# A fused attention and mixer kernel: idle transposes ahead of the first matmul, values loaded one key tile later, and the first weight loads three slots later

## The chip, the cores and the metric

The kernel runs on 1 core of one Trainium2 chip. The metric is device time in microseconds (us) of one execution; lower is better. Three plain runs give the time, and one further execution was profiled.

## The reference

Inputs q, k, v have the shape (4, 8, 576, 64): 4 batches, 8 heads, 576 tokens. Three stages follow one another.

```python
# 1. attention by positive random features (omega is 128 x 64)
q_s, k_s = q * D**-0.25, k * D**-0.25
def phi(x):
    h = einsum('bhsd,md->bhsm', x, omega) - (x * x).sum(-1, keepdims=True) / 2
    return exp(h - h.max(-1, keepdims=True)) / sqrt(128)
q_p, k_p = phi(q_s), phi(k_s)
kv, z = einsum('bhsm,bhsd->bhmd', k_p, v), k_p.sum(2)
x = einsum('bhsm,bhmd->bhsd', q_p, kv) / (einsum('bhsm,bhm->bhs', q_p, z) + 1e-6)
# 2. x as (4, 576, 512): token mixing, then a channel MLP of width 1536
u = x + (relu(x.T @ w_tok1) @ w_tok2).T
x = u + relu(u @ w_ch1) @ w_ch2
# 3. a 2D Fourier transform mixes x; layer norm; an MLP of width 2048
u = x + real(fft(fft(x, axis=1), axis=2))
out = u + relu(norm(u) @ w_ch1) @ w_ch2
```

## The kernel before

The order of all instructions is written out by hand, and each engine works through its own in that order. A single-precision matmul is made of three fast ones: each operand is split into a rounded high part and the rest.

The first 200 us are the attention stage. The 2304 tokens make 18 tiles of 128 tokens for the keys and 18 for the queries; every tile is worked in two groups of four heads, so `order` in `attention()` has 72 slots. Slots 0 to 9 are key tiles 0 to 4, two slots each; after that a slot of a key tile and a slot of a query tile alternate. In slot n the loop issues, in this order:

- `load`: the transfers of tiles that come up to six slots later, on SyncE's queue (SP). A key tile brings its values (`va`) with it, a split tile two pieces of them. The tiles rotate through three buffers, so a load waits until the tile three before it has been split.
- `project(n)`: six matmuls of 256 columns on TensorE (line 506), the tile's high and low part (`kh`, `kl`) times those of the scaled omega (`om_h`, `om_l`).
- `sums(n)`: for the key slot three before (`LAG`), four matmuls per batch and head with the values (line 540); `queries(n)`: for a query slot, four transposes of the features (line 565).
- `split_in`: the high part of a tile that comes four slots later, a cast on ScalarE (ACT) or for key tiles 1 and 3 on VectorE (DVE), then the low part on GpSimd (POOL), for key tile 0 on VectorE.
- `feature(n)`: the maximum on VectorE (`mx`, line 520), then the exponential on ScalarE (`f`): four activations straight from PSUM (line 524), or a subtraction on VectorE (`df`, line 527) and one wide activation (line 528).
- `results(n)`: numerators on TensorE (line 582) and the division on VectorE (lines 595 to 602).
- `side.step(...)`: work on the side. The later weights arrive in double precision, and `widen` takes each chunk apart into two single-precision parts: a load into `stg`, six wide VectorE operations (lines 341 to 372) and one on ScalarE (`cvy`, line 348), and a store. `weave` puts these items in one list; each item has a cost, each slot adds a budget to a credit, and items are issued while the credit pays for them. The first two loads of the list cost nothing, so they go out with the first step.

The identity for the transposes is made on GpSimd at the start. `bank("H")` hands out the two PSUM banks of that name in turn.

After the attention stage come the token mixing (lines 667 and 680), the channel MLP (lines 776 and 898), the Fourier stage and the last MLP (lines 1457 and 1470).

Of the kernel before, what the change touches and what calls it, by code (L numbers as in the profile page):

```python
# [9 lines left out]
F32 = mybir.dt.float32  # L10
# [10 lines left out]
B, H, S, D, M = 4, 8, 576, 64, 128  # L21
DM = H * D
NTOK = B * S
NT = NTOK // 128
# [2 lines left out]
BLK = 512  # L27

NWB = 3
NBLK = (NTOK + BLK - 1) // BLK  # L30

BLOCKS = [0, NBLK - 1, *range(1, NBLK - 1)]

SLOT0_US, SLOT1_US, SLOT_US, FIRST_US, SHORT_US, CH_US, FF_US, S_US, SAVED_US = 1.2, 0.45, 1.2, 3.9, 1.2, 4.3, 3.8, 1.6, 4.6


NP = NFF // 2
# [11 lines left out]
SPLIT = [i for i in range(NT) if i * 128 // S != (i * 128 + 127) // S]  # L51
# [140 lines left out]
def pieces(t0, n):  # L192

    done = 0
    while done < n:
        b, s = divmod(t0 + done, S)
        step = min(n - done, S - s)
        yield done, step, b, s
        done += step
# [103 lines left out]
def mix_kernel(ctx: ExitStack, tc: tile.TileContext, qt, kt, va, om, w1, w2, wch, wff, t1, t2, out):  # L303
    nc = tc.nc
    pe, act, dve, pool, sync = nc.tensor, nc.scalar, nc.vector, nc.gpsimd, nc.sync
# [7 lines left out]
    ident = const.tile([128, 128], F32, name="ident")  # L313
# [69 lines left out]
    def weave(chunks):  # L383


        items = []
        for i, ((_, done), work) in enumerate(chunks):
            if not i:
                items += [(0.0, chunks[c][0][0]) for c in range(2)] + work[:1]
            items += work[1:6]  # L390
            if i + 1 < len(chunks):
                items.append(chunks[i + 1][1][0])
            if i + 2 < len(chunks):
                items.append((0.0, lambda i=i: side.later(chunks[i + 2][0][0])))
            items.append(work[6])
            items.append((0.0, lambda done=done: side.later(done)))
        return items
# [5 lines left out]
    def slab(j):  # L403
        def store(st, free):
            kept[j] = dram.tile([128, 2, 1024], F32, name="kept")
            side.queue.dma_start(out=kept[j], in_=st["o"].bitcast(F32))
            whole.add(j)
            free()
        return widen(wch[j].bitcast(I32), 1024, store)
# [36 lines left out]
    def bank(tag):  # L446
        if tag not in pools:
            tag = "A"
        if tag == "A" and spare:

            tag = spare.pop(0)
            spare.append(tag)
        pl, bufs = pools[tag]
        return pl.tile([128, 512], F32, tag=tag, name=tag, bufs=bufs)
# [8 lines left out]
    ld = pl.enter_context(tc.tile_pool(name="ld", bufs=3))  # L463
# [5 lines left out]
    def projection():  # L469
        act.dma_start(out=om_sb, in_=om)  # L470
        act.mul(out=om_h, in_=om_sb, mul=scale)
        dve.scalar_tensor_tensor(out=om_l, in0=om_sb, scalar=scale, in1=om_h, op0=ALU.mult, op1=ALU.subtract)

    src = {}

    def load(kind, i):
        t = ld.tile([128, 4, 128], F32, tag="x", name=kind + "s", bufs=3)
        sync.dma_start(out=t, in_=(kt if kind == "k" else qt)[:, i])
        src[kind, i] = t
        if kind == "k":  # L480
            for part, row in enumerate([i] + [NT + c for c, j in enumerate(SPLIT) if j == i]):
                t = ld.tile([128, H, D + 1], F32, tag="v", name="v", bufs=6)
                sync.dma_start(out=t.rearrange("p h d -> p (h d)"), in_=va[row])
                src["v", i, part] = t

    def split_in(kind, i):
        t = src.pop((kind, i))
# [140 lines left out]
    def tok_weights():  # L628
        t1 = w1hl.bitcast(F32).rearrange("p a b c -> p a (b c)")
        t2 = w2hl.bitcast(F32).rearrange("p a b c -> p a (b c)")  # L630

        def done1(st, lo):


            o = st["o"].bitcast(F32)
            sync.dma_start(out=t1[:, :, lo:lo + 640], in_=o[:, :, 0:640])
            sync.dma_start(out=t1[64:128, :, 1280 + lo:1920 + lo], in_=o[0:64, :, 0:640])
            n = min(640, 1024 - lo)
            sync.dma_start(out=t1[0:64, :, 1536 + lo:1536 + lo + n], in_=o[64:128, :, 0:n])
            if n < 640:  # L640
                sync.dma_start(out=t1[0:64, :, 1280:1536], in_=o[64:128, :, n:640])

        def done2(st, lo):
            sync.dma_start(out=t2[:, :, lo:lo + S], in_=st["o"].bitcast(F32)[:, :, 0:S])

        def chunk(w, lo, n, done):
            return widen(w.bitcast(I32)[:, 2 * lo:2 * lo + 2 * n], n, lambda st, free: (done(st, lo), free()))

        return [chunk(w1, 0, 640, done1), chunk(w1, 640, 640, done1), chunk(w2, 0, S, done2), chunk(w2, S, S, done2)]
# [38 lines left out]
    def last_tile(b):  # L688
        return ((b + 1) * S - 1) // 128
# [3 lines left out]
    for b in range(B):  # L693
# [4 lines left out]
        c = [("k", i, g) for i in range(kn, ke) for g in range(2)]  # L698
# [7 lines left out]
    side = Side()  # L706
# [22 lines left out]
    def turns(n, c):  # L729
        return list(range(n)) if c % 2 == 0 else list(range(n))[::-1]  # L730
# [10 lines left out]
    def wait_whole(x):  # L741
        side.until(lambda: x in whole)

    PAIR1 = {(1, p_) for p_ in range(NP)}
    mix = Slots([j for c in range(NBLK) for j in turns(NCH, c)]
                + [(k, p_) for c in range(len(PLAIN)) for p_ in turns(NP, c) for k in (1, 2)],
# [6 lines left out]
    def operand():  # L753
        return [mlp0["ub"].tile([128, 4, BLK], F32R, tag=tag, name=tag) for tag in ("uh", "ul")]
# [26 lines left out]
    def attention():  # L781
        tiles = [(kind, i) for kind, i, g in order if g == (kind == "q")]
        at = {t: order.index(t + (int(t[0] == "q"),)) for t in tiles}
        late = {}
        n_all = len(order)

        def at_slot(n, kind):
            return order[n][1:] if 0 <= n < n_all and order[n][0] == kind else None

        def sums(n):  # L790
            if n in late:
                late.pop(n)()
            if (t := at_slot(n - LAG, "k")) is not None:
                parts = list(pieces(t[0] * 128, 128))
                kv_add(*t, parts[0])
                if len(parts) > 1:
                    late[n + 2] = lambda: kv_add(*t, parts[1])

        def queries(n):
            if (t := at_slot(n - LAG, "q")) is not None:  # L800
                turn(*t)
            t = at_slot(n - LAG_X, "q")
            if t is not None and t[1] == 0:
                turn_x(t[0], at_slot(n - LAG_NUM, "q") != (t[0] + 1, 0))
                for b in range(B):
                    if t[0] == last_tile(b):
                        fill.extend(tok_mix(b))

        def results(n):
            if (t := at_slot(n - LAG_NUM, "q")) is not None:  # L810
                numer(*t)
                divide(*t)
                if t[1] == 0:
                    split_x(t[0])

        loads, splits = list(tiles), list(tiles)
        for n in range(-1, n_all + LAG_X):
            while loads and at[loads[0]] <= n + AHEAD_LOAD:
                load(*loads.pop(0))
            if n == n_all:  # L820
                enter_mlp()
            if 0 <= n < n_all:
                project(*order[n])
            sums(n)
            queries(n)
            while splits and at[splits[0]] <= n + AHEAD_SPLIT:
                split_in(*splits.pop(0))
            if 0 <= n < n_all:
                feature(*order[n])
            results(n)  # L830
            if n >= 2:

                side.step(0.0 if n < 6 else SLOT0_US if n < 10 else SLOT1_US if n < 36 else SLOT_US)
            if fill and (len(fill) > 3 or n % 2 == 0):
                fill.pop(0)()
            for fn in early[:3]:
                fn()
            del early[:3]

    ctx.enter_context(tc.manual_schedule())  # L840
    projection()
    side.rest += weave(tok_weights() + [slab(j) for j in range(NCH)]
                       + [w(p_) for p_ in range(NP) for w in (first, second)])
    attention()
# [9 lines left out]
    wb = pm.enter_context(tc.tile_pool(name="wb", bufs=1, reuse_waits="tile"))  # L854
    mix.free.extend((wb, f"wb{i}") for i in range(NWB))

# [81 lines left out]
    def tables():  # L938
        sync.dma_start(out=t1_sb, in_=t1)
        pool.dma_start(out=t2_sb, in_=t2)  # L940
# [438 lines left out]
    tables()  # L1379
    for at_ in range(1, NBLK):  # L1380

# [8 lines left out]
        v = operand()  # L1390
        last = at_ + 1 == NBLK
        ch_block(at_, BLOCKS[at_], u, ff_prepare(0, v) if last else [lambda: ch_split(BLOCKS[at_ + 1], v)],
# [5 lines left out]
    v = mlp0["ub"].tile([128, 4, BLK], F32R, tag="uh", name="uh")  # L1398
    v = v[:, :, 0:BLK // 2], v[:, :, BLK // 2:BLK]
# [198 lines left out]
```

## Time and profile before

| | us |
|---|---|
| plain runs | 943.9, 944.2, 945.47 |
| median | 944.2 |
| profiled execution, its own time | 946.03 |
| its span, first to last instruction | 943.9 |
| mean granted TensorE clock over the span | 0.998 |

The span is what the trace shows; the profiled execution's own time is 2.1 us longer than its span and 1.8 us longer than the median of the plain runs. Positions in the trace are counted from the start of the span.

### The profile page before, as it was taken

The page shows a single profiled execution, that of the slowest core. Times are in us where ns is not written, and L with a number is a line of the kernel's source. Part 1 is how long each engine was busy: PE and PEld are TensorE (multiplying, and loading weights), DVE is VectorE, ACT ScalarE, POOL GpSimd, SP SyncE. Part 2 cuts the span into 40 slices and gives each one's busy share as a digit, 9 for nine tenths or more (in the row PEclk, how much of TensorE's full clock was granted, in tenths as well). Part 3 has the DMA queues.
Part 4 walks back from the last instruction along what each step waited for, and adds up shares of the span by engine and source line. Part 5 has one row for each costly group of instructions (what it writes and reads, how often), then busy time and mean ns, then how long its engine had stood idle before and what let it go on. Part 6 is the DMA issues. An engine that isn't in the chain of part 4 may idle for free.

```text
span 943.9 us, 14085 instructions
## 1 busy us (share of the span) xinstructions
PE 930.4 (99%) x5344; PEld 830.1 (88%) x5344; DVE 633.2 (67%) x1259; ACT 306.4 (32%) x709; POOL 120.7 (13%) x110
## 2 busy tenths in 40 slices
PE   7999999989999999999999999999999999999998
PEld 7999999978889888888888888889999998899986
DVE  5987999886776787877853667666565557533342
ACT  5886777721212322212221122222311113311121
POOL 3353444221211132011000000000000000000000
PEclk9999999999999999999999999999999999999999
DMA  7765554687897586583145358739766656677764
GB/s 268 231 211 177 184 213 160 252 301 258 345 411 318 174 310 236 180 302 135 60 174 213 134 185 270 240 112 386 268 229 234 227 190 226 227 263 253 249 213 151
DMA packets 68257, 216.47 MB, mean 229 GB/s; under 512 B 5600, under 2 KB 14432, under 8 KB 54240
## 3 DMA queue, kind: packets, MB, share of 16 engines
q1 hardware_dynamic: 60992, 172.40, 52.3%
q0 software_dynamic: 7056, 43.06, 12.3%
q8 instruction: 42, 0.69, 0.3%
q14 instruction: 23, 0.19, 0.1%
q10 hardware_dynamic: 144, 0.13, 0.0%
HBM read 169.30 MB, written 42.47 MB: 224 GB/s over the span
## 4 chain that ended last, share of the span: by engine, by line
PE 97%; DVE 2%; ACT 0%; DMA 0%; issue 0%; DVEq 0%; ACTq 0%
PE H L776 23%; PE A L898 16%; PE A L1470 14%; PE H L1457 12%; PE A L1264 7%; PE A L506 6%; PE H L540 4%; PE N L582 3%; PE A L565 2%; PE A L667 1%; PE A L680 1%; PE S L1077 1%; PE S L1090 1%; PE S L680 1%; PE H L667 1%; PE S L667 1%
## 5 line engine op out<-in xcount | busy, mean ns | idle before, releaser
L776 PE MATMUL H<-uh,w 128*128 128x512 f32 (+1 forms) x800 | 216.3, 356 | 2.1 <-DVE x L683 2.1
L776 PEld LDWEIGHTS H<-uh,w 128*128 128x128 f32 x800 | 137.3, 190 | 22.6 <-DVE x L683 2.3
L860 ACT ACTIVATE hh<-H 128x512 fp32r<-128x512 f32 (+1 forms) x92 | 49.1, 534 | 268.8 <-PE H L776 268.6
L776 PE MATMUL H<-ul,w 128*128 128x512 f32 (+1 forms) x304 | 114.2, 376 | 0.4 <-DVE ul L763 0.4
L898 PE MATMUL A<-hh,w 128*128 128x512 f32 (+1 forms) x480 | 108.7, 369 | 0.0
L1470 PE MATMUL A<-w2t,b 128*128 128x512 f32 x384 | 99.3, 394 | 0.0
L861 DVE SCALAR_TENSOR_TENSOR hl<-H,hh 128x512 fp32r<-128x512 f32 (+1 forms) x92 | 55.8, 606 | 63.8 <-ACT hh L860 63.7
L898 PEld LDWEIGHTS A<-hh,w 128*128 128x128 f32 x480 | 84.2, 188 | 15.0
L1457 PE MATMUL H<-b,w1t 128*128 128x384 f32 x480 | 91.4, 336 | 0.0
L1457 PEld LDWEIGHTS H<-b,w1t 128*128 128x128 f32 x480 | 85.0, 188 | 4.0 <-DVE tmp L1501 0.3
L1470 PEld LDWEIGHTS A<-w2t,b 128*128 128x128 f32 x384 | 70.6, 188 | 11.7
L524 ACT ACTIVATE f<-A,mx 128x128 f32<-128x128 f32 x240 | 69.8, 396 | 23.2 <-DVE mx L520 22.6
L776 PEld LDWEIGHTS H<-ul,w 128*128 128x128 f32 x304 | 57.6, 190 | 10.1 <-DVE ul L763 0.8
L898 PE MATMUL A<-hl,w 128*128 128x512 f32 (+1 forms) x240 | 59.3, 369 | 0.0
L1264 PE MATMUL A<-w,hh 128*128 128x512 f32 x192 | 50.5, 395 | 0.0
L520 DVE TENSOR_REDUCE mx<-A 128x4 f32<-128x512 f32 x70 | 47.7, 682 | 4.2 <-PE A L506 2.9
L898 PEld LDWEIGHTS A<-hl,w 128*128 128x128 f32 x240 | 42.5, 188 | 7.9 <-DVE hl L861 0.4
L540 PE MATMUL H<-v,f 128*128 128x65 f32 x320 | 40.3, 271 | 0.0
L1462 ACT ACTIVATE b<-tmp 128x384 fp32r<-128x384 f32 x16 | 8.4, 525 | 98.1 <-DVE tmp L1523 98.1
L360 DVE SCALAR_TENSOR_TENSOR cvo<-cvy,cvo 128x1024 int32<-128x1024 int32 (+2 forms) x32 | 39.7, 1241 | 0.5
L1264 PEld LDWEIGHTS A<-w,hh 128*128 128x128 f32 x192 | 34.6, 189 | 6.1
L540 PEld LDWEIGHTS H<-v,f 128*128 128x128 f32 x320 | 39.3, 192 | 0.2 <-DVE kvs L545 0.2
(261 smaller groups left out, 1688.8 us busy)
## 6 DMA issues: line engine op xcount, KB each, us to landing
w<-kept SPq DMA_DIRECT2D x60, 1024.0 KB, 6.5
w2t<-kept SPq DMA_DIRECT2D x55, 512.0 KB, 4.9
w1t<-kept SPq DMA_DIRECT2D x48, 512.0 KB, 5.0
stg<-in_wff_dram POOLq DMA_DIRECT2D x16, 1024.0 KB, 6.8
kept<-cvo POOLq DMA_DIRECT2D x13, 1024.0 KB, 6.4
stg<-in_wch_dram SPq DMA_DIRECT2D x9, 1024.0 KB, 6.3
kept<-cvo POOLq DMA_DIRECT2D x16, 512.0 KB, 7.4
kept<-so SPq DMA_DIRECT2D x16, 512.0 KB, 7.7
```

The lines of the kernel that those rows point to most:

```text
L360: dve.scalar_tensor_tensor(out=st["h"], in0=st["y"].bitcast(I32), scalar=-0x80000000, in1=st["h"], op0=ALU.bitwise_and, op1=ALU.bitwise_or)
L506: pe.matmul(out=pj[:, p_ * 256:p_ * 256 + 256], lhsT=a[:, c, :], rhs=w, start=(n == 0), stop=(n == 2), skip_group_check=True)
L520: dve.tensor_reduce(out=mx, in_=p4, axis=AX.X, op=ALU.max, negate=True)
L524: act.activation(out=f[:, hh], in_=p4[:, hh], func=AF.Exp, bias=mx[:, hh])
L540: pe.matmul(out=kvp[b, g][:, hh * 65:hh * 65 + 65], lhsT=ft["k", i, g][:, hh, :], rhs=src["v", i, int(off > 0)][:, 4 * g + hh, :], start=( ...
L776: pe.matmul(out=hb[:, 0:n], lhsT=w(a, kk), rhs=u[:, kk, 0:n], start=(c == 0), stop=(c == 11))
L860: act.activation(out=hh, in_=hb[:, 0:n], func=AF.Relu)
L861: dve.scalar_tensor_tensor(out=hl, in0=hb[:, 0:n], scalar=0.0, in1=hh, op0=ALU.max, op1=ALU.subtract)
L898: pe.matmul(out=acc[i][:, 0:cols], lhsT=a[:, cs], rhs=v, start=(n == 0 and c_ == 0), stop=(n == NCH - 1 and c_ == 2))
L1264: pe.matmul(out=acc[t], lhsT=a[:, t * 128:t * 128 + 128], rhs=w, start=(n == 0 and c_ == 0), stop=(n == NFF - 1 and c_ == 2))
L1457: pe.matmul(out=to, lhsT=w[:, a, cs], rhs=v[:, q], start=(start and n == 0), stop=(n == 5), skip_group_check=True)
L1470: pe.matmul(out=acc[t], lhsT=h[n // 2][:, t * 128:t * 128 + 128], rhs=w[:, n % 2], start=(begins and n == 0), stop=(ends and n == 2))
```

## The change

Three edits near the start, and one constant. Seventeen transposes of the identity are put on TensorE ahead of the attention loop, into a PSUM bank that nobody reads. `load` of key tile i brings the values of tile i - 1 (the last tile brings its own as well). `side.step` is called from slot 5 on instead of slot 2, with its budgets moved: none for four slots, 1.2 for four slots, then `SLOT1_US` up to slot 35, which grows from 0.45 to 0.55.

```diff
+IDLE = 17
-SLOT0_US, SLOT1_US, SLOT_US, FIRST_US, ... = 1.2, 0.45, 1.2, 3.9, ...
+SLOT0_US, SLOT1_US, SLOT_US, FIRST_US, ... = 1.2, 0.55, 1.2, 3.9, ...
...
         if kind == "k":
-            for part, row in enumerate([i] + [NT + c for c, j in enumerate(SPLIT) if j == i]):
-                t = ld.tile([128, H, D + 1], F32, tag="v", name="v", bufs=6)
-                sync.dma_start(out=t.rearrange("p h d -> p (h d)"), in_=va[row])
-                src["v", i, part] = t
+            values(i - 1)
+        if kind == "k" and i == NT - 1:
+            values(i)
+
+    def values(i):
+        if i < 0 or ("v", i, 0) in src:
+            return
+        for part, row in enumerate([i] + [NT + c for c, j in enumerate(SPLIT) if j == i]):
+            t = ld.tile([128, H, D + 1], F32, tag="v", name="v", bufs=6)
+            sync.dma_start(out=t.rearrange("p h d -> p (h d)"), in_=va[row])
+            src["v", i, part] = t
...
-            if n >= 2:
-                side.step(0.0 if n < 6 else SLOT0_US if n < 10 else SLOT1_US if n < 36 else SLOT_US)
+            if n >= 5:
+                side.step(0.0 if n < 9 else SLOT0_US if n < 13 else SLOT1_US if n < 36 else SLOT_US)
...
     projection()
+    idle = bank("H")
+    for _ in range(IDLE):
+        pe.transpose(idle[:, 0:128], ident, ident)
```

## Rows read from the trace of the kernel before

**Rows 1.** The page: busy time by engine, and the chain that ended last.

```profile
PE 930.4 (99%) x5344; PEld 830.1 (88%) x5344; DVE 633.2 (67%) x1259; ACT 306.4 (32%) x709; POOL 120.7 (13%) x110
...
PE 97%; DVE 2%; ACT 0%; DMA 0%; issue 0%; DVEq 0%; ACTq 0%
```

**Rows 2.** TensorE's waits, whole span: line, what it waited for, total, times, longest.

```profile
PE A L506 <- ACT kh L493: 5.3, 1, 5.3
PE H L776 <- DVE x L683: 2.1, 1, 2.1
```

**Rows 3.** The chain in order of time: start, length, what.

```profile
5.32 5.79 PE A L506 x24
11.11 1.04 PE H L540 x8
12.15 0.77 PE A L506 x6
12.92 0.84 PE H L540 x8
...
31.23 0.44 PE A L565 x4
```

**Rows 4.** Timeline of TensorE: start, length (pipelined, so longer than the spacing), what.

```profile
6.04 0.58 PE L506 MATMUL A<-om_h,kl 128*128 128x256 f32 x1
6.43 0.42 PE L506 MATMUL A<-om_h,kh 128*128 128x256 f32 x1
6.64 0.41 PE L506 MATMUL A<-om_l,kh 128*128 128x256 f32 x1
...
11.96 0.37 PE L506 MATMUL A<-om_h,kh 128*128 128x256 f32 x1
```

**Rows 5.** Stretches: length, busy time by engine, granted clock, DMA share, GB/s.

```profile
6.00:8.00 2.00, 2.00 (x10) 1.96 (x10) 1.02 (x2) 0.62 (x1) 1.39 (x2) 1.00 0.94 310
...
204.00:206.00 2.00, 2.00 (x7) 1.52 (x6) 2.00 (x2) 0.00 (x0) 0.00 (x0) 0.51 0.98 328
```

**Rows 6.** Timeline of GpSimd: the identity, and the low part of key tile 1.

```profile
1.23 0.29 POOL masks.py:199 TENSOR_SCALAR_AFFINE_SELECT ident<-ident 128x128 f32<-128x128 f32 x1
...
6.41 1.29 POOL L494 TENSOR_TENSOR kl<-ks,kh 128x512 fp32r<-128x512 f32 x1 [4.63 <-DVE kh L491]
```

**Rows 7.** Timeline of VectorE and then ScalarE, the features of slot 0.

```profile
7.30 0.69 DVE L520 TENSOR_REDUCE mx<-A 128x4 f32<-128x512 f32 x1 [0.98 <-PE A L506]
...
8.76 0.63 ACT L528 ACTIVATE f<-df 128x512 f32<-128x512 f32 x1 [0.94 <-DVE df L527]
```

**Rows 8.** Transfers issued from 9 to 10 us, and from 10 to 11 us: size, time to landing.

```profile
stg<-in_w_dram SPq DMA_DIRECT2D x2, 640.0 KB, 6.9
...
ks<-in_kt_dram SPq DMA_DIRECT2D x1, 256.0 KB, 7.6
```

**Rows 9.** Timelines of ScalarE and VectorE around the first widening.

```profile
17.80 0.62 ACT L493 CAST kh<-ks 128x512 fp32r<-128x512 f32 x1 [1.10 <-PE A L506]
...
20.63 0.75 ACT L348 ACTIVATE cvy<-cvy 128x640 f32<-128x640 f32 x1
...
21.42 0.50 DVE L356 TENSOR_SCALAR cvo<-cvy 128x640 int32<-128x640 int32 x1 [2.37 <-ACT cvy L348]
...
22.69 0.68 DVE L520 TENSOR_REDUCE mx<-A 128x4 f32<-128x512 f32 x1
```

**Rows 10.** Timeline of TensorE, the value matmuls of slot 11.

```profile
23.95 1.15 PE L540 MATMUL H<-v,f 128*128 128x65 f32 x8
24.91 0.36 PE L506 MATMUL A<-om_h,kh 128*128 128x256 f32 x1
```

**Rows 11.** The chain at the end of the attention stage.

```profile
202.22 4.60 PE H L776 x12
...
210.35 2.74 PE H L776 x12
```

**Rows 12.** VectorE's waits from 75 to 100 us.

```profile
DVE h1l L671 <- ACT h1h L670: 4.5, 2, 2.6
```

More of the change, by code (lines that the diff above doesn't have):

```diff
@@ L29 @@
 NWB = 3
+IDLE = 17
 NBLK = (NTOK + BLK - 1) // BLK
 BLOCKS = [0, NBLK - 1, *range(1, NBLK - 1)]
-SLOT0_US, SLOT1_US, SLOT_US, FIRST_US, SHORT_US, CH_US, FF_US, S_US, SAVED_US = 1.2, 0.45, 1.2, 3.9, 1.2, 4.3, 3.8, 1.6, 4.6
+SLOT0_US, SLOT1_US, SLOT_US, FIRST_US, SHORT_US, CH_US, FF_US, S_US, SAVED_US = 1.2, 0.55, 1.2, 3.9, 1.2, 4.3, 3.8, 1.6, 4.6
 NP = NFF // 2
```

## The prediction, made before the changed kernel was run

> **What bounds the kernel now.** I read the page first: TensorE is busy for 930.4 of 943.9 us, and the chain that ended last is 97% TensorE [rows 1]. So only time in which TensorE stands still, or runs slowly, can be won. Its list of waits says where it stands still: 5.3 us before the first matmul, which waits for the high part of key tile 0, and then almost nothing up to 2.1 us at the end of the attention stage [rows 2].
>
> Where it runs slowly is seen in the chain and the timeline. The first 24 projection matmuls take 5.79 us, 0.24 each, while six of them later take 0.77, 0.13 each [rows 3]. In the timeline they stand 0.21 us apart (6.43, 6.64) [rows 4]. 256 columns in 0.21 us are the lower of the two clocks, 1.2 GHz. The granted-clock column says 1.00 in that stretch [rows 5], so here it misses the low clock, and the spacing decides. TensorE did nothing before 5.32 us. The rise falls inside the first group of value matmuls: it takes 1.04 us, the next 0.84 [rows 3]. After that TensorE's work is a line without gaps, so a matmul that starts earlier moves the whole line, as long as features, tiles and weights keep up.
>
> **The change, part by part.** *The transposes.* The identity is finished at 1.23 + 0.29 = 1.52 us [rows 6], so TensorE can start at about 1.6. No transpose in this trace runs at the low clock. At the full clock four take 0.44 us, 0.11 each [rows 3]; twice that is 0.22, as for the matmuls. 17 of them fill 3.7 us and end at 5.3, just when the first projection starts now. Bounds: 17 x 0.11 = 1.9 us if the clock rises at once, and 17 x 0.41 = 7.0 us if cold transposes do not overlap at all (0.41 is the whole length of a cold matmul [rows 4]). I take 0.22: in the row the cold matmuls do overlap.
>
> When does the clock rise? Before, TensorE worked from 5.32 until some point between 11.11 and 11.96 [rows 3, 4], so 5.8 to 6.6 us. At the end of the attention stage it stood for 2.1 us, the clock fell (0.51 granted from 204 to 206 us [rows 5]), and twelve matmuls took 4.60 us in place of 2.74 [rows 11]; the excess of 1.86 is that of about 3.7 us at half clock. Counted from 1.6, the clock is up at 5.3 by the second row, and at 7.4 to 8.2 by the first.
>
> What the projections make of it: they don't shrink by half, because low parts are late. Key tile 0's is there at 6.04 in both kernels, its wait shows as the start of the third matmul [rows 4]; key tile 1's at 6.41 + 1.29 = 7.70 [rows 6], since neither the cast on VectorE nor the subtraction on GpSimd moves. With the full clock at 5.3, slot 0 ends at 6.04 + 4 x 0.117 = 6.5, slot 1 at 7.2, slot 2 waits for 7.7 and ends at 8.2, slot 3 at 8.9. (0.117 is the spacing at full clock: 0.77 over six less the start of a group.) The first value matmuls follow if the features of slot 0 are there: before they took 8.76 + 0.63 - 7.30 = 2.1 us from the end of the projection [rows 7], so 8.8 now: just in time. They end at 8.9 + 0.84 = 9.74, and slot 4 starts there in place of 11.96 [rows 4]: 2.2 us won. With the clock up at 7.4, slot 1 ends at 7.8 and slot 3 at 9.2: 1.9 us. Up at 8.2: 9.6, so 1.5 us. I take **2.0** (1.5 to 2.2).
>
> The Trainium skill (TensorE: Matmul & The Clock Gate, Part 1, "What's actually happening") says that the low clock is the state at rest, that activity releases it, and that the moment varies from run to run of the same kernel; it warns "don't fit to a specific cold count". By it the 24 cold matmuls are one draw; the trace, one execution, can neither confirm nor deny that. This speaks against my 2.0 and is a rival below.
>
> *Values one tile later.* On SP's queue, first k0, v0, k1, v1, k2, v2, it becomes k0, k1, v0, k2, v1. The omega comes on another queue beside the same amount of data: nothing. Tile 1 lands sooner, hidden behind VectorE's subtraction for tile 0. Tile 2 lands some 0.5 us sooner (one place in the queue), hidden because slot 4 wants it at 9.7. The values of tile i now have about five slots between issue and use, some 8 us at 0.77 + 0.84 = 1.61 us a slot [rows 3], against a landing of at most 7.6 for any tile [rows 8]: nothing; without that cover a late one would cost a few tenths. The first query load no longer stands behind the wait for a free values buffer.
>
> *First weight loads three slots later.* Now two of 640 KB stand in front of key tile 5's load, which is issued just after 10 us and needs 7.6 to land [rows 8], so past 17.6; ScalarE stands 1.10 us until 17.80 for it (the releaser named, TensorE, had long been done [rows 9]) and everything behind it is late: the features of slots 6 and 7, then the widening's activation at 20.63, for which VectorE stands 2.37 us, and so the maximum of slot 8 starts at 22.69 [rows 9], though at 1.61 us a slot that slot is projected by 12.15 + 4 x 1.61 + 0.77 = 19.4. TensorE feels the end of it: the eight value matmuls of slot 11 take 0.96 us (23.95 to 24.91 [rows 10]) in place of some 0.81, a loss of 0.15. The two slots after it lose about as much each: **0.5 us**, which could go. But in the new order the same activation stands behind the features of slot 10, and VectorE waits for it again, then catches up beside budgets of 0.55 in place of 0.45. From slot 12 on query slots lie between, so TensorE needs its features later: three slots take longer than the 4.8 us of the first ones. I take **0.3** of the 0.5. Bounds: 0.5 won, or the whole 2.37 laid on TensorE.
>
> *The budgets.* Up to slot 35 they sum to 4.8 + 23 x 0.55 = 17.45 in place of 4.8 + 26 x 0.45 = 16.5. One wide operation more is done before slot 36 and one fewer later. From 75 to 100 us VectorE waits 4.5 us for TensorE's token mixing [rows 12], so a backlog from the early slots is gone there, and time won passes on. At the end of the stage VectorE's chain sets the pace for some 17 us, and one wide operation more or fewer there is 1 us either way: taken as nothing.
>
> Sum: 2.0 + 0.3 = 2.3 us. Against the profiled execution: 946.03 - 2.3 = 943.7. Its own time is 1.8 above the median of the plain runs, so against that 944.2 - 2.3 = **941.9**, if the plain runs start as cold as the profiled one.
>
> **The rivals.** *The clock rises at another point in plain runs* (the page's rule). As a mechanism of this kernel: if before it is up after only 3.7 us of work, at 9.0, slot 2 is almost through at the low clock and slot 3 ends at 10.0, not 11.1. Now it ends at 8.9, so the transposes win 1.1, not 2.0: 944.2 - 1.1 - 0.3 = 942.8. For it: the plain runs are shorter than the profiled one, and the second row above. Against it: the one cold start seen.
>
> *VectorE eats it.* The 2.37 us at slot 10 delay slots 11 to 13 so far that TensorE waits for features until the old pace is reached: 944.2 - 2.3 + 2.0 = 943.9. For it: before, the same stall took TensorE's margin to zero. Against: the longer slots.
>
> *The end of the stage warms up.* With one wide operation fewer in VectorE's last chain TensorE stands less, and the clock doesn't fall: a further 1.86, so 940.0. Nothing in the trace says that it must.
>
> *Slower: a stall long enough for the clock to fall.* It decides when a stall at slots 12 to 14 reaches the 2.1 us after which the clock fell in rows 11. Then 2.37 of waiting and 1.86 of cold matmuls come on top: 944.2 - 2.3 + 4.2 = 946.1. Against it: the margin shown in rows 10 shrank to nothing, but no further. (That the transposes run into the first projection decides from 0.22 us each; even at 0.41 they end at 8.6, but then the clock is up, and slot 3 ends at 11.4 against 11.1: 944.5.)
>
> **How the numbers follow.** Forecast 0.50 (941.9, its own range 941.2 to 942.7); other rise of the clock 0.12; VectorE 0.20; warm end 0.10; slower 0.08. What a measurement can tell from no change is 0.2%, 1.9 us: faster is below 942.3, slower above 946.1. Faster: four fifths of the forecast and the warm end, 0.50. Same: the rest of the forecast and the two middle rivals, 0.42. Slower: 0.08. The range reaches from the warm end, 940.0, past the unchanged cases and a transpose overrun to 944.6; outside are the slow case and half of the warm one.
>
> **What would show it.** Transposes from 1.6 us, 0.22 apart, over by 5.4; projections of slot 1 at 0.117 from the start or from 8.2 at the latest; slot 4 at 9.7 to 10.5; key tile 5 landing in about 4 us; value matmuls from slot 11 on at 0.81 us per group and no TensorE wait for a feature before 75 us. It is wrong if the clock rises as late as before, if the first projection starts after 5.4, or if TensorE's waits grow by as much at 185 to 202 us.

## The result, and the profile after

The changed kernel takes 951.45 us (median of 5 runs, 949.99 to 952.13) against 944.25 before (943.9 to 945.49). The ratio, taken over all the runs and not from the two medians, is 1.0066, interval 1.0053 to 1.0080. It is slower by two thirds of a per cent, where 941.9 was forecast. Its profiled execution took 949.99 us, with a span of 947.8.

The page after:

```profile
PE 932.1 (98%) x5361; PEld 830.2 (88%) x5361; DVE 640.8 (68%) x1259; ACT 306.3 (32%) x709; POOL 114.9 (12%) x110
...
PE 90%; DVE 7%; ACT 1%; issue 1%; DMA 0%; POOL 0%; DVEq 0%; ACTq 0%
```

Against [rows 1] the same 1259 VectorE instructions are busy 7.6 us longer, and VectorE holds 7% of the chain that ended last, not 2%. TensorE's waits after (answering to [rows 2]): the wait before the first projection is gone, and waits for features (L532 is `f`) and for VectorE have come.

```profile
PE H L784 <- DVE x L691: 2.4, 1, 2.4
PE A L514 <- ACT f L532: 2.4, 5, 0.9
PE H L852 <- POOL ident masks.py:199: 1.6, 1, 1.6
PE N L624 <- DVE x L606: 1.4, 1, 1.4
PE A L573 <- ACT f L532: 1.1, 2, 0.7
PE A L573 <- DVE x L691: 0.9, 2, 0.5
```

The start, in TensorE's timeline, went as worked out (compare [rows 4]), and from 6.19 us on the matmuls stand 0.12 us apart, the higher clock:

```profile
1.58 3.80 PE L852 MATMUL H<-ident 128*128 128x128 f32 x17 [1.58 <-POOL ident masks.py:199]
5.24 0.39 PE L514 MATMUL A<-om_h,kh 128*128 128x256 f32 x1
...
6.30 0.28 PE L514 MATMUL A<-om_l,kh 128*128 128x256 f32 x1
6.42 0.28 PE L514 MATMUL A<-om_h,kl 128*128 128x256 f32 x1
...
8.98 1.00 PE L548 MATMUL H<-v,f 128*128 128x65 f32 x8
9.79 0.37 PE L514 MATMUL A<-om_h,kh 128*128 128x256 f32 x1
```

Slot 4 starts at 9.79 in place of 11.96. To see where the 2.2 us went, take the start of the first projection matmul of each slot from TensorE's timeline, changed kernel less kernel before:

| slot | 4 | 14 | 17 | 28 | 36 | 41 | 47 | 57 | 65 | 71 |
|---|---|---|---|---|---|---|---|---|---|---|
| us | -2.17 | -2.77 | -0.87 | -0.53 | -0.06 | +0.78 | +2.59 | +3.32 | +5.34 | +5.66 |

Three things happen. By slot 14 the start has won 2.8 us. By slot 36 all of it is gone. From there to slot 71 another 5.7 us are lost, in jumps. Slots 36 to 71 take 109.3 us in place of 103.6; this is the loss that makes the kernel slower.

The loss before slot 36 begins in VectorE's timeline, at the two places where it waits for ScalarE's scaling in the first two chunks (compare the one wait of 2.37 in [rows 9]):

```profile
22.96 0.49 DVE L357 TENSOR_SCALAR cvo<-cvy 128x640 int32<-128x640 int32 x1 [1.83 <-ACT cvy L349]
...
31.98 0.49 DVE L357 TENSOR_SCALAR cvo<-cvy 128x640 int32<-128x640 int32 x1 [1.80 <-ACT cvy L349]
```

The loss after slot 36 is seen when GpSimd's and VectorE's timelines are laid side by side. One group of subtractions on GpSimd, and VectorE beside it:

```profile
98.91 1.30 POOL L502 TENSOR_TENSOR kl<-ks,kh 128x512 fp32r<-128x512 f32 x1 [6.80 <-ACT kh L501]
100.47 1.97 POOL L617 TENSOR_TENSOR xl<-x,xh 128x512 fp32r<-128x512 f32 x1 [0.26 <-ACT xh L616]
102.40 2.28 POOL L502 TENSOR_TENSOR ql<-qs,qh 128x512 fp32r<-128x512 f32 x1
```

```profile
99.23 2.06 DVE L361 SCALAR_TENSOR_TENSOR cvo<-cvy,cvo 128x1024 int32<-128x1024 int32 x1
...
102.18 1.34 DVE L365 SCALAR_TENSOR_TENSOR cvo<-cvo,stg 128x1024 f32<-128x1024 int32 x1
103.44 1.79 DVE L369 TENSOR_SCALAR cvy<-cvo 128x1024 int32<-128x1024 int32 x1
...
106.68 0.68 DVE L342 TENSOR_SCALAR cvy<-stg 128x1024 f32<-128x1024 f32 x1
...
108.58 1.22 DVE L373 SCALAR_TENSOR_TENSOR cvo<-cvo,cvy 128x1024 fp32r<-128x1024 f32 x1
```

An operation of the kind of L361 or L373 takes 1.22 us by itself, and 2.06 when it starts at 99.23, inside `kl`, which ends at 100.21. One of the kind of L369 or L342 takes 0.68 by itself, and 1.79 when it meets `ql`. GpSimd's own 1.30 grow to 1.97 and 2.28. The kernel before, in the same place:

```profile
98.27 1.94 DVE L360 SCALAR_TENSOR_TENSOR cvo<-cvy,cvo 128x1024 int32<-128x1024 int32 x1
...
101.10 1.34 DVE L364 SCALAR_TENSOR_TENSOR cvo<-cvo,stg 128x1024 f32<-128x1024 int32 x1
...
103.90 0.68 DVE L368 TENSOR_SCALAR cvy<-cvo 128x1024 int32<-128x1024 int32 x1
```

```profile
97.82 1.31 POOL L494 TENSOR_TENSOR kl<-ks,kh 128x512 fp32r<-128x512 f32 x1 [5.30 <-ACT kh L493]
99.38 1.99 POOL L609 TENSOR_TENSOR xl<-x,xh 128x512 fp32r<-128x512 f32 x1 [0.24 <-ACT xh L608]
101.31 2.29 POOL L494 TENSOR_TENSOR ql<-qs,qh 128x512 fp32r<-128x512 f32 x1
```

Its subtractions run from 97.82 to 103.60 us. Two wide operations meet them, as in the changed kernel; the third, of line 368, stands one slot later, behind a division, and takes its 0.68. The order of items, which follows from their costs and the budgets in the code, says the same:

```
slot   kernel before       changed kernel
 42    high                high
 43    low                 low, unit          <- unit (L368, now L369) meets ql
 44    unit                take
 45    take                scaled, rest
``` 

To put a number on it, take each wide operation of the widening between 10 and 220 us, its duration less the shortest of the same line and size. In the kernel before, the 41 that overlap a subtraction have 12.6 us of such excess, the 54 others 0.2. In the changed kernel it is 20.9 for 39 that overlap, and 0.15 for 56 that don't. The difference, 8.3, is about VectorE's added busy time.

### The profile page after: what moved, and what is told of

It reads as the page before. It is cut to its first block, busy times and chain, and to the rows that moved or that the text cites. A ratio compares the mean times of both kernels' runs of the same rounds, so it can differ in the third digit from the quotient of the medians.

```text
span 947.8 us, 14120 instructions
## 1 busy us (share of the span) xinstructions
PE 932.1 (98%) x5361; PEld 830.2 (88%) x5361; DVE 640.8 (68%) x1259; ACT 306.3 (32%) x709; POOL 114.9 (12%) x110
## 4 chain that ended last, share of the span: by engine, by line
PE 90%; DVE 7%; ACT 1%; issue 1%; DMA 0%; POOL 0%; DVEq 0%; ACTq 0%
PE H L784 22%; PE A L909 16%; PE A L1481 14%; PE H L1468 12%; PE A L1275 7%; PE A L514 4%; PE H L548 2%; PE N L590 2%; PE A L675 1%; PE S L1088 1%; PE A L573 1%; DVE mx L528 1%; PE S L1101 1%; DVE cvo L373 1%; PE S L688 1%
## 5 line engine op out<-in xcount | busy, mean ns | idle before, releaser
L532 ACT ACTIVATE f<-A,mx 128x128 f32<-128x128 f32 x240 | 69.7, 391 | 29.8 <-DVE mx L528 26.6
L361 DVE SCALAR_TENSOR_TENSOR cvo<-cvy,cvo 128x1024 int32<-128x1024 int32 (+2 forms) x32 | 41.9, 1310 | 0.4
L373 DVE SCALAR_TENSOR_TENSOR cvo<-cvo,cvy 128x1024 fp32r<-128x1024 f32 (+2 forms) x32 | 41.1, 1285 | 0.0
```

The lines of the kernel that those rows point to most:

```text
L361: dve.scalar_tensor_tensor(out=st["h"], in0=st["y"].bitcast(I32), scalar=-0x80000000, in1=st["h"], op0=ALU.bitwise_and, op1=ALU.bitwise_or)
L373: dve.scalar_tensor_tensor(out=st["o"][:, 1, 0:n], in0=st["l"].bitcast(F32), scalar=2.0 ** -52, in1=st["y"], op0=ALU.mult, op1=ALU.mult)
L532: act.activation(out=f[:, hh], in_=p4[:, hh], func=AF.Exp, bias=mx[:, hh])
```

## The experiments

Five rounds each, beside runs of the kernel before on the same chip. The table has the slot starts (less those of the kernel before), the length of slots 36 to 71, the excess as above, and the medians. All but the medians and ratios are read from the one profiled execution of each run. Theory A, at first: where the widening's items stand against the slots makes the loss. B: the late start of the side work makes it. C: TensorE's earlier start itself does.

| run | slot 4 | slot 17 | slot 36 | 36 to 71 | excess | median | ratio, interval |
|---|---|---|---|---|---|---|---|
| changed kernel | -2.2 | -0.9 | -0.1 | 109.3 | 20.9 | 951.45 | 1.0066 (1.0053 to 1.0080) |
| 1 transposes only | -2.0 | +2.1 | +2.5 | 103.5 | 12.7 | 950.49 | 1.0049 (1.0030 to 1.0069) |
| 2 equal budget | -2.1 | -0.8 | -0.3 | 103.5 | 12.6 | 944.5 | 0.9999 (0.9991 to 1.0008) |
| 3 budget only | 0.0 | +1.6 | +1.6 | 109.4 | 20.7 | 955.15 | 1.0113 (1.0098 to 1.0127) |
| 4 no transposes | -1.1 | +0.2 | +1.0 | 109.4 | 21.0 | 952.65 | 1.0077 (1.0065 to 1.0089) |
| 5 changed, no low parts | -2.0 | -0.5 | +0.2 | 102.6 | 2.8 | 941.38 | 0.9959 (0.9947 to 0.9972) |
| 6 before, no low parts | -0.9 | -0.4 | -0.4 | 102.2 | 2.5 | 941.71 | 0.9962 (0.9949 to 0.9974) |
| 7 values as before | -1.8 | -0.4 | +0.1 | 103.6 | 12.7 | 945.63 | 1.0005 (0.9996 to 1.0014) |
| 8 spread start | -1.6 | -2.4 | -0.4 | 103.5 | 15.6 | 943.63 | 0.9991 (0.9982 to 1.0000) |
| 9 spread, pattern | -1.8 | -2.5 | -0.5 | 105.1 | 9.0 | 946.75 | 1.0019 (1.0010 to 1.0028) |
| 10 before, pattern | -0.2 | -0.4 | -0.4 | 105.2 | 6.1 | 946.68 | 1.0022 (1.0013 to 1.0031) |
| 11 pattern early | -1.9 | -2.6 | -0.4 | 105.1 | 8.9 | 946.7 | 1.0016 (1.0007 to 1.0025) |
| 12 changed, pattern | -1.9 | -0.6 | +0.2 | 107.3 | 9.1 | 948.39 | 1.0042 (1.0030 to 1.0055) |
| 13 spread, no early low | -1.8 | -2.6 | -2.6 | 103.5 | 11.6 | 942.45 | 0.9973 (0.9963 to 0.9984) |
| 14 spread, less VectorE | -1.9 | -2.6 | -2.4 | 103.5 | 14.0 | 942.09 | 0.9970 (0.9960 to 0.9979) |

**1. The transposes alone**

```diff
     projection()
+    idle = bank("H")
+    for _ in range(17):
+        pe.transpose(idle[:, 0:128], ident, ident)
```

> The kernel before with the 17 transposes alone; loads, values and budgets stay. Theory A (the place of the widening's items against the slots sets the loss: with one item more issued before slot 36, VectorE's wide operations meet GpSimd's subtractions more often): items stand as before, so no loss, and what is left of the 2.2 us of the start after VectorE's early backlog: 942 to 944. Theory B (the shifted work makes the loss because it starts late and comes up against the end of the early slots; the place matters little): 942, as the widening starts as early as before. Theory C (TensorE's earlier start itself makes VectorE late everywhere): 948 to 951.

950.49 us: slower, which no theory had for this reason. Slots 36 to 71 are as before, so A holds there; the loss is early. Key tile 5's load, still behind the two of 640 KB, is issued at 10.06 us (10.05 before), though all of TensorE's work in front of it is now 2 us earlier. It even lands later, after 8.7 us in place of 7.6; the loads behind it now go out 2 us sooner (its values at 11.78, not 13.79), but that these slow it is not shown. ScalarE's and VectorE's timelines, where [rows 9] had 1.10 and 2.37:

```profile
18.91 0.62 ACT L493 CAST kh<-ks 128x512 fp32r<-128x512 f32 x1 [3.92 <-PE A L506]
...
22.52 0.49 DVE L356 TENSOR_SCALAR cvo<-cvy 128x640 int32<-128x640 int32 x1 [5.42 <-ACT cvy L348]
```

The 2 us won at the start turn into 3 us of added wait on both engines. TensorE waits for features, 1.2 us before 20.11 and 1.4 us before 24.99, and then its clock falls: the granted clock is 0.50 from 28 to 30 us, and eight value matmuls take 1.80 us in place of 1.00. Slot 17 starts 2.1 us late.

```profile
26.92 1.80 PE L540 MATMUL H<-v,f 128*128 128x65 f32 x8
```

```profile
28.00:30.00 2.00, 2.00 (x11) 2.00 (x11) 1.97 (x5) 1.96 (x6) 1.46 (x1) 0.50 0.00 0
```

That is the prediction's slow rival, a stall long enough for the clock to fall, in this kernel and not in the changed one. From slot 4 to slot 14 it costs 4.2 us, the rival's price, though neither wait reaches the 2.1 us that the rival asked for. The trace explains only part of the median: its execution took 946.78 us at a mean granted clock of 0.998, while the four longer ones, 949.76 to 952.33, had 0.991 to 0.995. An estimate: 0.006 of 945 us is 5.7 us of TensorE's work, about what they are longer. Where the clock fell in them no trace shows.

**2. Equal budget**

```diff
-SLOT0_US, SLOT1_US, ... = 1.2, 0.55, ...
+SLOT0_US, SLOT1_US, ... = 1.2, 0.509, ...
```

> The changed kernel with the fourth budget at 0.509 in place of 0.55: the budgets up to slot 35 sum to 16.5 as before, and from slot 34 on each slot issues the same items as the kernel before; transposes, later values and later first loads stay. Theory A: the loss of 5.7 us between slots 36 and 71 goes, the excess of wide operations that overlap a GpSimd subtraction falls from 20.9 to about 12.6 us, time 943 to 945.5. Theory B: the late start stays, so 949 to 951. Theory C: 949 to 951.

944.5 us, slots 36 to 71 in 103.5, excess 12.6: A as expected. B and C fall as causes of the big loss, since the late start and the transposes are still there. No gain is left either.

**3. Budget alone**

```diff
-SLOT0_US, SLOT1_US, ... = 1.2, 0.45, ...
+SLOT0_US, SLOT1_US, ... = 1.2, 0.4866, ...
```

> The kernel before with the third budget at 0.4866 in place of 0.45: one item more before slot 36, and from slot 34 on the same items in each slot as the changed kernel; no transposes, no later values, no later loads. Theory A: the loss appears without anything else of the change: 949 to 952, excess of wide operations about 20 us. Theories B and C: 944 to 945.

955.15 us: the loss appears in the kernel before, from one constant. 109.4 us for slots 36 to 71, excess 20.7. It loses 1.6 more in the early slots, so it is slower than A said. The profiled execution took 953.07 at a granted clock of 0.998, the three others 955.12 to 956.38 at 0.995 or 0.996. By that some 2 us of the median may be the clock's and not the order's.

**4. The changed kernel without the transposes**

```diff
-IDLE = 17
+IDLE = 0
```

> The changed kernel without the transposes; everything else of it stays. Theory A: the loss stays and the gain of the start goes: 950 to 953. Theory B: 951 to 953, too. Theory C: back to 944 to 946.

952.65 us: C falls again. Without the transposes the changed kernel's slots 17 to 36 start 1.1 us later; by the ratios it is 1 us, inside their intervals.

**5 and 6. GpSimd's subtractions taken away** from about slot 30 on, in the changed kernel and in the one before; the high part stands in for the low part there.

```diff
+        bare = i >= (11 if kind == "k" else 7)
+        l = h if bare else ld.tile(..., name=kind + "l")
...
+        if not bare:
             (dve if (kind, i) == ("k", 0) else pool).tensor_tensor(out=l, in0=t, in1=h, op=ALU.subtract)
...
-        xl = xs.tile([128, DM], F32R, tag="xl", name="xl")
+        xl = xh if i >= 3 else xs.tile([128, DM], F32R, tag="xl", name="xl")
...
+        if i < 3:
             pool.tensor_tensor(out=xl, in0=x[:, 0:DM], in1=xh, op=ALU.subtract)
```

> The changed kernel without GpSimd's subtractions from about slot 30 on (key tiles 11 to 17, query tiles 7 to 17, attention tiles 3 to 17: the high part is used in place of the low part, so the result of these is less exact); TensorE's and VectorE's instructions stay the same. Theory A1 (the loss is the stretching of VectorE's wide operations while GpSimd subtracts): the operations of 1024 take their short times, slots 36 to 71 take 103 us or less in place of 109.3, and no more than the same in the kernel below; time 941 to 945. Theory A2 (two wide operations in one slot make VectorE late, whatever GpSimd does): slots 36 to 71 still take 3 us or more longer than in the kernel below; 947 to 950.

> The kernel before, without the same subtractions of GpSimd (key tiles 11 to 17, query tiles 7 to 17, attention tiles 3 to 17 use the high part in place of the low part). Slots 36 to 71 took 103.6 us with them. Theory A1: 102.5 to 103.6, and the wait at the end of the stage gets shorter; 941 to 944.5. Theory A2: the same in this kernel; it is the difference to the run above that tells the two apart.

The two kernels, 7 us apart, come to 941.38 and 941.71. Slots 36 to 71 take 102.6 and 102.2: the changed order costs 5.7 us with GpSimd's subtractions (109.3 less 103.6) and 0.4 without. The groups of wide operations of line 361 (360 in the kernel before) from 75 to 185 us; the columns are busy time, mean ns, idle before. First the kernel before, then the changed one, then run 5:

```profile
L360 DVE SCALAR_TENSOR_TENSOR cvo<-cvy,cvo 128x1024 int32<-128x1024 int32 x7 | 9.9, 1421 | 0.0
```

```profile
L361 DVE SCALAR_TENSOR_TENSOR cvo<-cvy,cvo 128x1024 int32<-128x1024 int32 x7 | 12.3, 1751 | 0.0
```

```profile
L361 DVE SCALAR_TENSOR_TENSOR cvo<-cvy,cvo 128x1024 int32<-128x1024 int32 x7 | 8.5, 1215 | 0.0
```

**7. Values with their own tile again**, equal budget, against the kernel before:

```diff
+    idle = bank("H")
+    for _ in range(17):
+        pe.transpose(idle[:, 0:128], ident, ident)
...
-SLOT0_US, SLOT1_US, ... = 1.2, 0.45, ...
+SLOT0_US, SLOT1_US, ... = 1.2, 0.509, ...
...
-            if n >= 2:
-                side.step(0.0 if n < 6 else SLOT0_US if n < 10 else SLOT1_US if n < 36 else SLOT_US)
+            if n >= 5:
+                side.step(0.0 if n < 9 else SLOT0_US if n < 13 else SLOT1_US if n < 36 else SLOT_US)
```

> The changed kernel with the fourth budget at 0.509 and with the values loaded together with their own key tile, as before: transposes and later first loads alone. If the later values matter only through the first tiles (0.6 us of landing, hidden): the same as with them, slot 4 at 9.8 to 10.0, 943 to 945.5. If they are what keeps the early slots from waiting: TensorE waits at slots 11 to 14 as with the transposes alone, 946 to 950.

945.63 us, beside 945.34 for the kernel before: like run 2. The later values matter little; what keeps the early slots from the wait of run 1 is that the big loads go out later: key tile 5 lands in 4.4 us here.

**8. Spread start**

```diff
-SLOT0_US, SLOT1_US, ... = 1.2, 0.55, ...
+SLOT0_US, SLOT1_US, ... = 0.6, 0.6134, ...
```

> The changed kernel with the budgets 0.6 (slots 9 to 12) and 0.6134 (slots 13 to 35) in place of 1.2 and 0.55: they sum to 16.5 as before and the items stand as before from slot 34 on, but the first chunk is issued one operation a slot, so that VectorE's size operation comes a slot after ScalarE's scaling and does not wait for it. Theory A with the stall at slots 14 to 17 as the second loss: that stall (1.9 us) goes, 2.2 us or more of the start reach slot 36, time 941 to 943. If the stall has another cause: 943.5 to 945.5, as with equal budgets alone.

The stall at slots 14 to 17 goes (-2.4 at slot 17, still -2.4 at slot 28), and no wait for the scaling is left in VectorE's list. But between slots 28 and 36 the lead shrinks to 0.4, not the 2.2 or more that were expected to arrive. 943.63 us; the interval just reaches 1. VectorE in that stretch meets GpSimd:

```profile
54.89 1.55 DVE L369 TENSOR_SCALAR cvy<-cvo 128x576 int32<-128x576 int32 x1
...
58.02 1.12 DVE L342 TENSOR_SCALAR cvy<-stg 128x576 f32<-128x576 f32 x1
```

**9 to 12. A pattern that avoids GpSimd**: the budget of two slots at once in the two slots of four in which GpSimd does not subtract, from slot 36 to 59; run 11 from slot 16 on.

```diff
-... SLOT1_US if n < 36 else SLOT_US)
+... SLOT1_US if n < 36 else SLOT_US if n >= 60 else 2 * SLOT_US * (n % 4 < 2))
```

> The run with the spread start (budgets 0.6 and 0.6134), and from slot 36 to 59 the budget of 1.2 a slot is given as 2.4 in two slots of four and nothing in the two in which GpSimd subtracts (slots with n mod 4 of 2 and 3). The sum stays. If meeting GpSimd is what the wide operations lose by: the excess of those that overlap falls from 15.6 to 11 us or less, slots 36 to 59 get shorter, 941 to 943. If two wide operations in one slot cost more than they save: 944 to 948.

> The kernel before with the same pattern of budgets from slot 36 to 59, nothing else. By the meeting with GpSimd: the excess falls from 12.6 to 9 us or less, 942.5 to 944.5. By the crowding of two in a slot: 945 to 949.

> As the first run of this call, with the pattern from slot 16 on (1.2268 in two slots of four, nothing in the other two). With the spread start TensorE was 2.4 us ahead at slot 28 and lost 2.0 of it by slot 34, beside wide operations of 1.55 and 1.12 us that overlapped GpSimd's subtractions. If these are the cause: more than 1.5 us ahead at slot 36, 940.5 to 942.5. If it is the sum of VectorE's work: no better than the first run.

> The changed kernel with the pattern of budgets from slot 36 to 59, its sum and its early slots as they are. If the change lost its time by meeting GpSimd's subtractions: the excess falls from 20.9 to 14 us or less and the 5.7 us lost between slots 36 and 71 shrink to 2 or less: 944 to 947. If the cause is only how many items stand before slot 36: 949 to 952.

The excess falls as meant, to 6 to 9 us, and in the changed kernel two of the 5.7 lost us come back (107.3); 3.7 stay, so run 12 lies between its two expectations. In run 11 the lead at slot 36 is 0.4, no more than in run 8. And 9, 10 and 11 are slower than without the pattern, by 1.6 us in slots 36 to 71. Two slots' wide operations in one slot hold up the maxima and divisions behind them; run 10 shows TensorE's wait for the division at 1.7 us where it was 1.0:

```profile
PE N L616 <- DVE x L598: 1.7, 2, 1.0
```

So crowding has a price too, and fewer meetings alone do not make a better order.

**13 and 14. What eats the lead before slot 36?** Run 13 is run 8 without GpSimd's subtractions of key tiles 6 to 10, query tiles 2 to 6 and attention tiles 0 to 2; run 14 is run 8 without the operation of line 361 in the four token chunks.

```diff
+        bare = 6 <= i <= 10 if kind == "k" else 2 <= i <= 6
...
+            if n == 1024:
                 dve.scalar_tensor_tensor(out=st["h"], ...)
```

> The run with the spread start, without GpSimd's subtractions of key tiles 6 to 10, query tiles 2 to 6 and attention tiles 0 to 2 (the high part stands in for the low part), so from slot 14 to about slot 32; from there on all as it was. It was 2.4 us ahead of the kernel before at slot 28 and 0.4 at slot 36. If the lead is lost where wide operations meet GpSimd: 2.4 to 3 us ahead at slot 36, 940.5 to 942. If it is lost because VectorE simply has too much work before slot 36: less than 1.2 us ahead, 943 to 944.

> The run with the spread start, without one wide operation (line 361) of each of the four first chunks, some 3 us of VectorE's work before slot 34 (the token weights lose their sign); GpSimd works as it did. If VectorE's amount of work before slot 36 eats the lead: 2 us or more ahead at slot 36, 941 to 942.5. If it is the meeting with GpSimd alone: less than 1.2 us ahead, 943 to 944.

Either brings the whole lead, 2.6 and 2.4 us, through slot 36 to the end: 942.45 and 942.09 us against 945.01. They do not tell the two reasons apart; they show that relief of either kind is enough. That VectorE is at its limit there fits, but is not shown by itself. Both leave work out. Of the kernels that leave none out, run 8 is the fastest, 0.1% ahead at best.

## Why the prediction was wrong

**The start: right, in part by luck.** 17 transposes from 1.58 to about 5.2 us, the wait for key tile 1's low part to 7.70, slot 4 at 9.79 (9.74 forecast). The clock came by the shorter of the two rows. The Trainium skill's warning on cold counts (TensorE: Matmul & The Clock Gate, Part 1, "What's actually happening") is borne out by the traces: the rise varies from execution to execution. The runs with all of the transposes have slot 4 between -2.2 and -1.6. Run 6, which starts like the kernel before, has its projections 0.12 us apart from 9.55 us on and slot 4 at 11.06, not 11.96; in run 4, without transposes, it is at 10.90. Against run 4 the transposes win 1.1 us, which is what the rival "the clock rises at another point" gave them; the 2.2 is won against the late rise of the one execution profiled before.

**Key tile 5: right.** It landed in 3.9 us, and the losses at slots 11 to 13 went; 0.6 in place of 0.3 by slot 14. That edit is also what keeps the transposes from harming, which the prediction did not see: run 1.

**VectorE's early waits: the rival came true.** "VectorE eats it" had 0.20 and 943.9. The scaling of the first chunk is waited for again, and the one of the second too; TensorE waits for features at slots 15 to 17, and by slot 36 the lead is 0.06. Run 8 loses the lead some slots later; only runs 13 and 14, which leave work out, keep it.

**The budgets: the step that failed.** "One wide operation more or fewer there is 1 us either way: taken as nothing." I read the 0.95 as an amount of work. It is a phase: of the 48 wide operations of slots 36 to 70, 39 come a slot or two earlier. The trace of before had GpSimd's subtractions and VectorE's wide operations, but I never laid them side by side; its wide operations of one line and size took 0.68 us here and 1.78 there, and that was the hint. The term measured +5.7 us in place of 0 (runs 2, 3, 5 and 6). None of the prediction's three signs of being wrong looks at slots 36 to 71.

**VectorE's waits from 75 to 100 us** [rows 12] were read as room in which a backlog vanishes. The first jumps, at slots 41 and 47, lie in that stretch and right behind it, so it did not take them up.

**The end of the stage.** The warm rival's number came too, but not by its mechanism: TensorE stood 2.4 us, longer than the 2.1 before, and in this execution the clock stayed up all the same.

```profile
206.00:208.00 2.00, 0.09 (x1) 0.09 (x1) 2.00 (x5) 0.00 (x0) 1.01 (x1) 1.00 0.68 180
```

The twelve matmuls that took 4.60 us in [rows 11] took 3.06. That gave 1.8 us back: +5.66 at slot 71, +3.9 in the span. It is not the change's doing: among the profiles, runs 1 and 2 have 3.0 us there and runs 7 and 8 have 4.5, and a kernel's times often lie in two groups some 1.6 us apart. The record tells the groups apart by the mean granted clock: of the 27 executions of the kernel before beside runs 9 to 12, the 17 at 0.999 or 1.000 took 943.48 to 944.64 us, the 10 at 0.998 took 945.15 to 945.92.

## What to carry to other kernels

A budget that spreads side work over slots sets a phase, not only an amount: before changing one, list which item falls into which slot, and hold it against the slots in which another engine works in the same memory. When an edit adds to such a sum, give it back elsewhere (0.509 for 0.55 was worth 6 to 7 us) before judging the rest of the change. And a transfer that does not land sooner turns an earlier start into a longer wait, in run 1 one after which the clock fell: a gain ahead of it is real only if the transfer moves too.

## What the hardware showed

Wide VectorE operations and GpSimd's subtractions do not share, they take turns. At 98.27 us of the kernel before, a 1.2 us operation takes 1.94 because `kl` still runs; `xl`, started at 99.38, takes 1.99 in place of 1.30 as it then waits in turn. Over the stage, excess is 12.6 us where they overlap and 0.2 where they don't; the maxima, which read PSUM, kept their 0.68 us throughout. The Trainium skill (SBUF — State Buffer, "SBUF: two separate sides") has the mechanism: VectorE and GpSimd share one pair of ports, held for the whole instruction by whoever starts first, while the other "fully blocks"; it names VectorE operations with two inputs in SBUF and those in a two-port mode. The trace agrees, up to 1.1 us a meeting; which mode an operation ran in no run here shows. The prediction would have needed it: by that rule the place of the wide operations is a term of the sum.

Transposes alone bring TensorE's clock up: in run 14 they start 0.21 us apart at first and the last ones 0.11 (4.61, 4.72, 4.83 us), before any other work of that engine. The granted-clock column does not show the low clock at the start of an execution: in the changed kernel too it reads 1.00 from 2 to 4 us, where the transposes start 0.21 us apart.
